# DeltaNet attention and a multiplicative FFN on one core: the 1382 hand-listed steps put in a new order

## The chip, the cores and the metric

The kernel runs on one core of one Trainium2 chip. The metric is the device time of one execution in microseconds (us), lower is better. It is given as the median of several runs; the profile is one further execution. PE stands for TensorE's products, PEld for its weight loads, DVE for VectorE, ACT for ScalarE, POOL for GpSimd and SP for SyncE, which issues nearly all DMAs here.

## The reference

```python
def _attn_ref(q, k, v, beta):            # (4, 8, 768, 48) each, beta (4, 8, 768)
    k_n = k / (np.linalg.norm(k, axis=-1, keepdims=True) + 1e-06)
    state = np.zeros((B, H, D, D))
    for t in range(S):
        kt, vt, bt = k_n[:, :, t], v[:, :, t], beta[:, :, t, None]
        y[:, :, t] = np.einsum('bhd,bhde->bhe', q[:, :, t], state)
        v_old = np.einsum('bhde,bhd->bhe', state, kt)
        state = state + bt[:, :, :, None] * np.einsum('bhd,bhe->bhde', kt, vt - v_old)

x = y.transpose(0, 2, 1, 3).reshape(3072, 384)
a, b = x @ w1, x @ w2                    # (384, 1024) each
out = ((a * b) @ w3) @ w_out             # (1024, 1024), (1024, 384)
```

All values are fp32; w1, w2, w3 and w_out arrive as float64.

## The kernel before

**Stages.** The 768 tokens are cut into 12 chunks m of 64, handled in pairs j (or units u) of two. All 4 batches and 8 heads of a chunk are worked on together, so its products are many small ones, with at most 64 rows and 64 columns of weights, side by side in the 128x128 array. The FFN's products are large ones with 128x128 weights. Since (h @ w3) @ w_out = h @ (w3 @ w_out), `fold` multiplies the two weights once. Each part of the program is a Python generator; one call of it up to its next `yield` is a **step**. `ORDER` is a text that names the part of each step from first to last, so "the third c5" in it is the third step of `chain(5)`. Every engine runs its instructions in the order in which the steps issue them (`in_text_order`): nothing is moved at run time, and an instruction that waits holds up all behind it on its engine.

**The names in `ORDER`:**

- k, q, v (L1223 and after): load a chunk of keys, queries or values by SP. K, Q (`by_tensor`, L369): transpose them by TensorE, then two steps that copy the results out of PSUM by DVE or ACT. From chunk 4 on p (`load_perm`, L261) issues 16 DMAs in two steps and d (`by_vector`, L355) transposes in four steps on DVE.
- g (`squares`): four times a square on POOL and a sum on DVE, then a small product that adds across halves; N (`norms`): some fifteen short DVE instructions and another such product. beta: its load and transposition.
- s (`scores`, for chunks 0 and 1 `first_scores`): products of keys with keys and queries in two halves, each read by DVE into U (L463 or L420) and PT (L474); h (`first_queries`) is the second half's work for chunks 0 and 1. u (`to_blocks`) stores U to DRAM in four DMAs.
- V (`inverse`): fetches U of a pair as 32x32 blocks (for the first pair a DVE transposition, L505, in its place) and inverts them on DVE in 31 steps of two instructions (L524, L529); the result goes out by DMA (L549), for the first pair by four DVE transpositions (L533).
- e (`corner`): fetches the inverses (eight DMAs; for the first pair a product and two ACT copies), a DVE transposition (L602), a product (the third step; L619), two ACT copies, a second product (the fifth step), two ACT copies.
- c (`chain`): the recurrence. Step 1: product with the state; 2: R on DVE (L706); 3: product with the inverse; 4: X on DVE (L717); 5: product with the keys; 6: the new state on DVE (L738). For chunk 0 steps 1 and 2 fall away.
- y (`outputs`): products for the chunk's result (L777), four ACT copies (L795), and DMAs that fill xT.
- P (`piece`): one piece of a weight: DMA (L838), two ACT instructions (L846, L849), one on DVE (L851), one on POOL (L853), which join the float64 halves into fp32. P0-7 are w_out, P8-23 w3, P24-35 w1 and w2. t (`transpose_w3`): four TensorE transpositions and an ACT copy. f (`fold`): 8 large products in two halves and a copy; f0 needs t0 and t1, f1 t2 and t3, and so on.
- a, b (`ab`, L934; a23 is unit 2, columns 3): product with w1, ACT copy, product with w2, multiplication on DVE. For the last unit a5 is `features` (L1074), a Strassen form on the sums of X and W.
- S (`slab_sums`, POOL; DVE for the last unit), o (L1166; seven products of a Strassen form with the folded weight), x (`result`: ACT and DVE read the banks of o, SP stores). T: sums of the folded weight on POOL.

A token whose generator is already at its end does nothing.

**PSUM.** Two double banks (tag "w") serve the attention's products in turn, four banks (tag "f") the large ones and the transpositions. A step that takes a bank waits until its last content has been read.

**The order before** starts with keys and scores, then mixes weight pieces, V0 and `fold`; from about 100 us on it alternates between runs of `ab` or single products of `o` and small products of e, c, s and y.

Of the kernel before, what the change touches and what calls it, by code (L numbers as in the profile page):

```python
# [1358 lines left out]
```

## Time and profile before

| | before |
|---|---|
| time, median of 3 runs | 556.68 us (556.57 to 558.01) |
| span of the profiled execution | 556.1 us |
| `ab`, L934: busy, two groups of 288 records | 106.9 and 106.7 us |
| `o`, L1166: the two largest groups, 320 and 240 records | 57.3 and 42.8 us |
| `fold`, L913 | 43.5 us |
| V on DVE, L524 and L529 with Vb | 43.0 and 43.0 us |
| DMA queue q1 (SP's and ACT's) | 52.56 MB, 46.3% of 16 engines |

A group's line has the source line, engine, operation, tiles and shapes, then busy time and mean length, then the idle time of the engine before these instructions and what ended it. A large matrix product stands as two records. In the chain of waits each piece is a stretch of work that had to end before the next could start.

### The profile page before, as it was taken

To read this page: it belongs to the slowest core of one execution; us is meant where nothing else is said; L and a number is where in the kernel's file an instruction comes from. 1 tells how busy PE (TensorE), PEld (TensorE's weight loads), DVE (VectorE), ACT (ScalarE), POOL (GpSimd) and SP (SyncE) were. 2 spreads that over 40 slices of the span, in tenths; PEclk is the share of its full clock that TensorE was granted. 3 is DMA by queue.
4 is the path that set the end of the run, shared out by engine and by line. 5 is a ranking of instruction groups with operands and counts; after the bars stand their busy time and mean duration, and the time that the engine had idled before them with its cause. 6 is when DMAs were issued, how large, how long until landed. Compare 5 with 4: busy or idle time off the path is not lost.

```text
span 556.1 us, 19932 instructions
## 1 busy us (share of the span) xinstructions
PE 533.6 (96%) x8732; PEld 390.8 (70%) x8732; DVE 343.7 (62%) x800; ACT 145.7 (26%) x291; POOL 169.7 (31%) x213
## 2 busy tenths in 40 slices
PE   6699999999999999999999999999999999989997
...
PEclk9999999999999999999999999999999999999999
...
GB/s 189 339 307 230 158 140 150 128 160 55 96 48 55 119 147 72 67 88 89 122 74 100 70 91 80 126 38 83 51 15 154 26 60 38 18 58 1 0 2 57
DMA packets 191527, 54.22 MB, mean 98 GB/s; under 512 B 178928, under 2 KB 185072, under 8 KB 191440
## 3 DMA queue, kind: packets, MB, share of 16 engines
q1 hardware_dynamic: 189328, 52.56, 46.3%
...
q10 hardware_dynamic: 2112, 0.39, 0.5%
q14 instruction: 19, 0.16, 0.1%
...
## 4 chain that ended last, share of the span: by engine, by line
PE 93%; DVE 3%; issue 2%; DMA 2%; ACT 0%; SPq 0%; DVEq 0%
PE ps_f L934 38%; PE ps_f L1166 20%; PE ps_f L913 7%; PE ps_w L672 6%; PE ps_w L777 4%; PE ps_f L1074 4%; PE ps_w L619 3%; PE ps_w L1074 2%; PE ps_w L451 2%; PE ps_f L369 1%; PE ps_w L457 1%; PE ps_f L904 1%; DMA beta_fm<-in_beta_dram 1%; PE ps_w L409 1%; PE ps_w L1166 1%
## 5 line engine op out<-in xcount | busy, mean ns | idle before, releaser
L934 PE MATMUL ps_f<-xT,w2s 128*128 128x512 f32 (+1 forms) x288 | 106.9, 524 | 0.0
L934 PE MATMUL ps_f<-xT,w1s 128*128 128x512 f32 (+1 forms) x288 | 106.7, 524 | 0.0
L934 PEld LDWEIGHTS ps_f<-xT,w2s 128*128 128x128 f32 x288 | 54.1, 190 | 46.5 <-issue 41.6
L934 PEld LDWEIGHTS ps_f<-xT,w1s 128*128 128x128 f32 x288 | 54.0, 190 | 45.3 <-issue 41.6
L1007 POOL TENSOR_TENSOR ab<-ab 128x256 f32<-128x256 f32 x80 | 56.4, 731 | 78.7 <-DVE ab L950 73.8
L946 ACT COPY ab<-ps_f 128x512 f32<-128x512 f32 (+1 forms) x48 | 24.3, 515 | 134.4 <-PE ps_f L934 130.3
L1166 PE MATMUL ps_f<-w,ab 128*128 128x192 f32 x320 | 57.3, 332 | 1.9 <-DVE osb L1197 1.3
L1166 PEld LDWEIGHTS ps_f<-w,ab 128*128 128x128 f32 x320 | 51.6, 190 | 3.3 <-issue 2.4
L524 DVE TENSOR_TENSOR tb<-Vb,Ub 128x31 f32<-128x31 f32 (+15 forms) x124 | 43.0, 347 | 15.4 <-DMA Ub<-Ud 11.5
L529 DVE TENSOR_TENSOR Vb<-Vb,tb 128x31 f32<-128x31 f32 (+15 forms) x124 | 43.0, 346 | 4.3
L913 PE MATMUL ps_f<-wo,w3T 128*128 128x384 f32 x128 | 43.5, 491 | 0.4 <-ACT w3T L907 0.4
L1166 PE MATMUL ps_f<-room,ab 128*128 128x192 f32 x240 | 42.8, 332 | 0.0
L950 DVE TENSOR_TENSOR ab<-ab,ps_f 128x512 f32<-128x512 f32 (+1 forms) x48 | 27.4, 589 | 24.0 <-PE ps_f L934 24.0
L1166 PEld LDWEIGHTS ps_f<-room,ab 128*128 128x128 f32 x240 | 38.7, 190 | 0.7
L913 PEld LDWEIGHTS ps_f<-wo,w3T 128*128 128x128 f32 x128 | 23.5, 190 | 15.4 <-ACT w3T L907 0.5
L301 POOL TENSOR_TENSOR sq<-ktok 128x384 f32<-128x384 f32 x24 | 19.7, 835 | 43.5 <-DMA out_dram<-osb 16.9
L658 POOL TENSOR_TENSOR vtok<-vtok,n 128x384 f32<-128x384 f32 x24 | 19.8, 832 | 39.5 <-DMA vtok<-in_v_dram 39.5
L635 ACT COPY T<-ps_w 32x512 f32<-32x512 f32 x24 | 13.8, 577 | 67.2 <-PE ps_w L619 46.2
L795 ACT COPY xT<-ps_w 112x256 f32<-112x256 f32 x48 | 14.3, 384 | 65.0 <-PE ps_w L777 61.7
L451 PE MATMUL ps_w<-KQ 48*64 48x128 f32 x320 | 21.9, 274 | 1.8 <-DVE PT L474 1.5
L717 DVE TENSOR_TENSOR X<-ps_w,wt 128x768 f32<-128x768 f32 x12 | 11.5, 956 | 19.4 <-PE ps_w L672 12.9
L1197 DVE TENSOR_TENSOR room<-room,ps_f 128x384 f32<-128x384 f32 (+1 forms) x13 | 7.0, 537 | 26.4 <-PE ps_f L1166 26.4
...
## 6 DMA issues: line engine op xcount, KB each, us to landing
...
```

The costliest lines, as they stand in the source:

```text
L451: pe.matmul(ps[half(z), 0, n : n + 128], lhsT=x[:, 0, :], rhs=x.rearrange("p j t -> p (j t)"), start=True, stop=True,)
L524: dve.tensor_tensor(out=tv, in0=V[:, 0 : s + 1, s : s + 1].to_broadcast([P, s + 1, n]), in1=U[:, s, s + 1 : BS].unsqueeze(1).to_broadcast( ...
L529: dve.tensor_tensor(out=o, in0=o, in1=tv, op=ALU.subtract)
L672: pe.matmul(out(ps, r, h, z), lhsT=lhs(r, h, z), rhs=rhs(r, h, z), start=True, stop=True,)
L777: i = pe.matmul(region(h, z, r), lhsT=lhs, rhs=rhs, start=part[n] not in part[:n], stop=part[n] not in part[n + 1 :],)
L913: pe.matmul(ps[:, 0:DM], lhsT=w3Ts[jc, kc // 4][:, kc % 4 * P : kc % 4 * P + P], rhs=wo(kc), start=(kc == 0), stop=(kc == KF - 1),)
L934: pe.matmul(ps[:].rearrange("p b c t -> p b (c t)"), lhsT=w[:, m, js], rhs=x[:, m, :, c0:c1].rearrange("p b c t -> p b (c t)"), start=(m = ...
L946: act.copy(out=t, in_=ps)
L950: dve.tensor_tensor(out=t, in0=t, in1=ps, op=ALU.mult)
L1007: (dve if u == last else pool).tensor_tensor(out=o_, in0=x_, in1=y_, op=op)
L1074: pe.matmul(ps[:, j, :], lhsT=w[j], rhs=x, start=first and j == 0, stop=j == 1, skip_group_check=not first,)
L1166: pe.matmul(ps[b][:, b, :], lhsT=ab_of(u, HF * f + i, t0), rhs=ws_[w][:, i], start=first and i == 0 and (b == 0 or n == "F"), stop=i == HF ...
```

## The change

The text of `ORDER` is replaced by another arrangement of the same 1382 tokens. Each part's own steps stay in their order; no part, tile, shape or instruction is added or taken away. What moves with a step is all that it issues, its DMAs too. At the start the two chunks of keys come first, weight pieces follow with their four steps together, and K1's copies stand behind P12, P0, P3 and P9. Later, small steps that stood one or two at a time between large products are more often in one row, and large products likewise. The diff, cut to its core (the lines that hold the steps spoken of below):

```diff
 ORDER = """
-k0 g0 g0 g0 K0 V0 g0 k1 P12 K0 K0 beta K1 P0 g0 g0 K1 K1 g0 q1 P12 g0 P12 P12 beta g0 g0 beta N0
-P8 P9 P8 P8 P8 P3 P0 P3 P3 P9 P0 s1 s1 s1 P9 s0 P3 P0 P13 P13 P13 s0 s0 V0 V0 V0 P1 P1 Q1 P1 P9
-Q1 P10 P13 V0 V0 Q1 P1 P10 P2 P2 t0 t0 P2 P4 P4 V0 t1 P2 t1 V0 P4 P4 h1 t4 t4 N0 P6 f0 P7 P10
-P10 P5 t2 t5 P18 V0 V0 P11 P6 V0 P6 P6 N0 P16 P19 V0 P7 P7 P5 P5 P5 q0 V0 t5 h1 P18 f2 P11 V0
...
-t9 v0 V0 P23 f4 f4 t14 f4 t15 t15 P21 P15 P15 t7 q3 V0 v1 Q2 Q2 V0 e0 h0 h0 e0 Q2 g1 e0 g1 t7 g1
-f3 e0 e0 K2 P27 K2 e1 e0 e0 n0 e1 k3 f7 P27 n0 e1 c0 e1 P21 e1 f7 V1 g1 c0 y0 P28 c0 P20 P25 f7
-P20 P20 P29 f3 P33 y0 n1 n1 P21 g1 c0 c1 y0 g1 g1 K2 f3 P28 P28 P28 P34 c1 t13 t13 t12 t12 P25
...
-n3 V1 V1 b2 a00 a00 a05 a05 g2 g2 g2 g2 a06 n2 b1 b1 b0 e2 b0 a06 g2 b3 b3 b7 b7 o0 g2 c2 n3 x0
-e2 e2 g2 g2 o0 d4 e2 g2 e2 g2 o0 S0 S0 S0 e2 c2 d4 S0 S0 e3 S0 S0 x0 S0 S0 S0 S0 e3 e3 S0 S0 d4
...
-S1 n5 n4 a13 a12 a12 a13 V2 e4 a17 e4 a11 g3 g3 g3 g3 a11 Q3 c4 g3 g3 n4 c4 e4 a16 a16 e5 e4 e4
-e4 o1 x1 S1 a17 S1 S1 S1 e5 e5 S1 e5 d6 n5 g3 c4 c4 g3 o1 S1 c4 V3 c4 g3 e5 e5 o1 p7 g3 N3 c5 p7
-x1 S1 x1 S1 y4 S1 y4 c5 o1 d7 d7 d7 d7 s7 s7 k8 g4 s7 s7 s6 s7 s7 u7 s6 s6 s6 s6 s6 c5 S1 c5 o1
...
-V3 e6 g4 a26 a26 a26 a24 d8 a21 n6 c6 e6 a26 d8 e7 a24 e6 e6 p9 g4 g4 g4 s8 N4 s8 a23 a23 s8 e6
-S2 e7 a21 e6 a23 a23 c6 e7 e7 c6 v7 o2 v9 o2 n7 n7 S2 y6 S2 S2 S2 V4 x2 K2 N4 c6 c6 o2 y6 e7 S2
-S2 S2 d9 d9 p10 S2 e7 c7 S2 x2 o2 d9 d9 c7 S2 s8 c7 x2 s8 o2 s8 c7 S2 y7 S2 v8 n8 x2 K1 o2 x2 x2
-u8 Q2 s9 s9 S2 S2 s9 y7 y7 s9 s9 u9 S2 o2 x2 s9 c7 x2 c7 V4 a32 a32 N4 k10 x2 x2 a36 a36 d10 d10
...
-e10 e11 e11 W x4 e11 c10 o4 S4 N5 e11 c10 c10 e11 c10 S4 S4 o4 x4 y10 S4 c11 n11 o4 S4 y10 n11
-c11 c11 c11 S4 S4 o4 y11 x4 S4 y11 y11 S4 x4 o4 S4 x4 x4 x4 x4 x4 o4 x4 a50 a50 a51 X5 a52 X5
...
+k0 K0 k1 K1 K0 K0 g0 g0 g0 g0 V0 g0 g0 g0 g0 P12 P12 P12 P12 beta P0 P0 P0 P0 P3 P3 P3 K1 beta
+beta P9 P9 P9 P9 P3 K1 K1 K1 g0 g0 N0 s1 t4 P13 P13 P13 P13 P1 P1 P1 P1 s1 s1 t4 s0 s0 s0 P2 P2
+P2 P2 P10 P10 P10 P10 t1 t1 t5 t5 V0 V0 q1 Q1 Q1 Q1 f2 h1 P8 P8 P8 P8 t0 V0 V0 V0 V0 V0 P4 P4
+P4 P4 P6 P6 P6 P6 t2 V0 V0 V0 t0 f0 P5 P5 P5 P5 P7 P7 P7 P7 f2 V0 P18 P18 P18 P18 V0 V0 V0 V0
...
+h0 V0 V0 e0 e0 e0 e0 e0 k2 K2 K2 K2 K2 g1 P28 g1 g1 P23 P21 g1 k3 g1 Q0 P26 P20 g1 n0 K3 K3 K3
+e0 e0 e1 P21 t15 t15 f7 f7 e1 e1 e1 P20 t12 g1 g1 g1 P25 q3 P25 P25 P25 P30 v1 P27 P27 P27 P30
+P30 P30 c0 f7 e1 e1 e1 t12 Q3 g1 c0 c0 y0 y0 c0 c1 t13 t13 f6 P27 P35 n1 n1 c1 N1 P26 c1 s2 P29
+Q3 Q3 P35 P35 c1 P24 P29 P29 P24 P24 s2 f6 f6 s2 P33 P33 P31 N1 N1 s2 s2 s2 y1 P31 y1 s3 P32
+P32 s3 s3 s3 k5 y0 y0 P24 b0 b0 s3 s3 P29 b4 b4 P34 P34 P33 u2 u3 c1 b6 b3 b1 b6 b1 y1 P35 P34
...
+T T v2 n2 n2 b1 p4 p4 d4 k4 g2 a04 d4 g2 g2 g2 T T S0 b1 g2 g2 g2 a05 a05 S0 a06 b7 a07 a06 c1
+b7 a07 g2 V1 V1 o0 V1 v3 e2 e2 e2 d4 e2 d4 g2 g2 N2 c2 c2 e2 e2 o0 x0 o0 p5 e3 e3 e3 S0 S0 S0
...
+o1 x1 e4 a14 S1 S1 S1 a17 S1 S1 S1 n4 S1 g3 g3 d6 d6 c4 c4 e5 e4 e4 e4 e5 o1 e5 c4 N3 e5 e5 e5
+c4 c4 c4 y4 y4 c5 n5 S1 o1 x1 c5 c5 p7 d7 p7 d7 d7 d7 N3 c5 v6 n6 s7 s7 s7 s7 s7 s7 o1 s6 s6 p8
+u7 x1 v7 s6 s6 s6 u6 o1 S1 S1 S1 S1 S1 S1 x1 N3 n7 S1 S1 s6 V3 V3 y5 y5 y5 c5 c5 o1 x1 x1 x1 x1
+V3 V3 p8 k9 V3 V3 V3 V3 c6 d8 d8 x1 o1 x1 x1 V3 V3 V3 V3 V3 V3 V3 V3 V3 V3 V3 V3 d8 V3 V3 a22
...
+g4 g4 N4 a22 a22 e6 s8 s8 s8 e6 e7 e7 a26 a26 S2 S2 a23 a23 S2 o2 S2 x2 S2 S2 S2 c6 c6 N4 s8 s8
+s8 u8 o2 c6 c6 y6 y6 p9 p9 e7 c7 e7 e7 v9 S2 n9 e7 o2 x2 c7 N4 d9 d9 V4 S2 S2 S2 S2 p10 k10 o2
+d9 d9 c7 c7 s9 y7 y7 y7 s9 s9 d10 d10 o2 x2 x2 s9 s9 u9 c7 o2 x2 x2 x2 a30 V4 x2 S2 S2 S2 o2 x2
...
+e8 e8 a37 S3 g5 g5 N5 n8 c8 c8 e8 e8 e8 o3 o3 x3 S3 S3 e9 e9 d10 e9 e9 c8 c8 o3 e9 x3 e9 S3 S3
...
+e11 N5 N5 e10 c10 o4 x4 x4 S4 S4 e11 e11 e11 S4 W S4 W S4 S4 c10 c10 c10 S4 S4 S4 S4 S4 S4 S4
+S4 W S4 S4 o4 c11 n11 c11 e11 o4 e11 c11 c11 y10 y10 y11 y11 y11 x4 o4 x4 x4 o4 x4 x4 x4 x4 x4
...
 """
```

More of the change, by code (lines that the diff above doesn't have):

```diff
@@ L76 @@
-c9 y8 y8 K1 S3 S3 c9 c9 o3 N5 o3 x3 s10 d11 s10 s10 y9 s10 s10 d11 d11 d11 S3 S3 W y9 y9 S3 S3
-o3 x3 W s10 x3 x3 s11 s11 s11 s11 s11 u10 u11 V5 S3 S3 x3 x3 o3 x3 x3 a44 s11 v11 V5 a45 V5 V5
-V5 V5 a45 a42 a42 v10 V5 a44 a46 a46 V5 V5 V5 V5 V5 V5 a41 V5 V5 V5 V5 a43 c9 a43 V5 V5 a41 a47
-a47 V5 V5 a44 a44 V5 V5 V5 V5 W V5 a40 a40 a45 V5 a43 V5 a41 V5 V5 V5 V5 a43 a45 a42 a40 a42 c9
-a46 V5 e10 e11 e10 W a41 W a40 c10 n10 n10 c10 e10 N5 a47 e10 e10 W a46 S4 a47 S4 S4 o4 S4 S4 S4
-e10 e11 e11 W x4 e11 c10 o4 S4 N5 e11 c10 c10 e11 c10 S4 S4 o4 x4 y10 S4 c11 n11 o4 S4 y10 n11
@@ new lines @@
+P34 P33 V1 V1 b3 b6 P32 b6 b5 b5 P31 V1 V1 V1 V1 V1 V1 V1 V1 V1 V1 V1 V1 V1 y1 a06 a06 a05 a05
+a03 a03 b7 b7 a00 a00 a07 a07 V1 V1 V1 P31 P32 b0 b0 b4 b4 b3 b3 a01 a01 a01 a02 V1 V1 V1 V1 V1
+a01 V1 a03 a03 V1 V1 V1 a00 a00 b2 a02 b2 a02 a02 V1 V1 V1 V1 V1 V1 V1 b2 b2 b5 b5 a04 a04 a04
+T T v2 n2 n2 b1 p4 p4 d4 k4 g2 a04 d4 g2 g2 g2 T T S0 b1 g2 g2 g2 a05 a05 S0 a06 b7 a07 a06 c1
+b7 a07 g2 V1 V1 o0 V1 v3 e2 e2 e2 d4 e2 d4 g2 g2 N2 c2 c2 e2 e2 o0 x0 o0 p5 e3 e3 e3 S0 S0 S0
+S0 c2 c2 o0 x0 e3 e3 e3 c2 c2 S0 S0 S0 S0 S0 S0 S0 S0 S0 S0 o0 x0 x0 n3 n3 c3 c3 y2 y2 p5 d5 c3
@@ new lines @@
+p11 d11 d11 y9 y9 y9 s10 s10 u10 s10 o3 x3 x3 x3 s11 s11 x3 s11 s11 S3 s11 u11 V5 o3 x3 x3 V5
+V5 V5 V5 V5 V5 V5 V5 V5 a46 a46 a47 a47 v10 a43 a43 V5 s11 V5 V5 V5 V5 V5 V5 V5 V5 V5 V5 V5 V5
+V5 V5 V5 a45 a45 a41 a41 a40 a44 a44 a40 a42 a40 a42 a42 a42 a40 V5 V5 V5 V5 a41 a44 a44 V5 V5
+V5 x3 e10 a41 a45 a46 a46 a43 a43 o4 a45 x4 c9 e10 e10 e10 a47 c9 e10 c10 a47 o4 n10 n10 c10
+e11 N5 N5 e10 c10 o4 x4 x4 S4 S4 e11 e11 e11 S4 W S4 W S4 S4 c10 c10 c10 S4 S4 S4 S4 S4 S4 S4
+S4 W S4 S4 o4 c11 n11 c11 e11 o4 e11 c11 c11 y10 y10 y11 y11 y11 x4 o4 x4 x4 o4 x4 x4 x4 x4 x4
```

44 lines of the change are left out of this document (19 added, 25 removed).

## The prediction, made before the result was known

> **What bounds the kernel now.** I read the page first: engines, slices, chain.
>
> ```profile
> PE 533.6 (96%) x8732; PEld 390.8 (70%) x8732; DVE 343.7 (62%) x800; ACT 145.7 (26%) x291; POOL 169.7 (31%) x213
> PE   6699999999999999999999999999999999989997
> PE 93%; DVE 3%; issue 2%; DMA 2%; ACT 0%; SPq 0%; DVEq 0%
> ```
>
> TensorE (PE) is the bound: it is busy nearly everywhere after the first two slices, and 93% of the chain that ended last is its products. The same products run after the change, so only three things can move: what a change between large and small products costs, what is lost before PE is full, and the stalls behind that. 3% of the chain, some 17 us, is DVE. The span is 556.1; the median of the runs shown is 556.68, so I add 0.6 to a span to get a time.
>
> **Part one: the changes.** I marked every step of both lists that issues products and counted where large (128x128 weights) and small (at most 64x64) ones follow each other: 109 times before, 85 after, so 24 fewer, or 12 round trips. The chain of waits and PE's timeline price a round trip:
>
> ```profile
> 359.31 20.80 PE ps_f L934 x48
> 380.80 2.77 PE ps_f L934 x6
> 435.87 0.87 PE ps_w L672 x64
> ```
>
> ```profile
> 391.57 0.94 PE L672 MATMUL ps_w<-X,ktok 64*48 64x48 f32 x64
> 392.33 0.77 PE L619 MATMUL ps_w<-T,T 33*33 33x32 f32 x64
> ```
>
> Columns of the chain: start, length, what. Eight halves of `ab`, six records each, take 20.80 in one piece; a half alone between small products takes 2.77. With n for a half and d for entering and leaving, 8n+d=20.80 and n+d=2.77, so n=2.576 and **d=0.19**. On the small side a product of `chain` alone takes 0.87, but 392.33-391.57=0.76 when another small one follows: **0.11** more for leaving. Together 0.30 per round trip. Twelve make **-3.6** us. The large side alone would give -2.3; a change that falls where PE waits anyway saves nothing. I take 3.6, since PE waits little.
>
> **Part two: the start.** What PE must issue ahead of the first product of `corner` (e0) I add up from the chain's rows:
>
> ```profile
> 14.90 2.06 PE ps_w L409 x122
> 16.96 4.42 issue
> ...
> 32.45 7.74 PE ps_f L913 x24
> ...
> 40.63 1.04 PE ps_f L369 x64
> ...
> 45.28 0.44 PE ps_f L904 x4
> ...
> 63.09 0.56 PE ps_w L563 x8
> ```
>
> A half of `fold` takes 2.58 (a third of 7.74), four transpositions of w3 0.44, a set of 64 small ones 0.93 (1.04 less the 0.11), a score 2.06. Before: ten halves, fourteen sets of four, seven of 64, two scores and 1.5 for beta and sums, 44.1 us in all. e0 starts at 63.0, so 18.9 us are lost by then. In the new list two more halves and one set less stand ahead of it: 48.8.
>
> ```profile
> 10.13 0.59 ACT L379 COPY KQ<-ps_f 112x512 f32<-112x512 f32 x1 [1.77 <-PE ps_f L369]
> ...
> 16.11 0.68 ACT L846 ACTIVATE w<-raw 128x512 f32<-128x512 f32 x1 [4.27 <-DMA raw<-in_moe_w_dram]
> 16.69 0.66 ACT L849 ACTIVATE raw<-raw 128x512 uint32<-128x512 uint32 x1
> ```
>
> ```profile
> 13.05 0.20 DVE L310 TENSOR_SCALAR seed<-ss 128x32 uint32<-128x32 uint32 x1
> ...
> 16.38 0.19 DVE L334 TENSOR_TENSOR wt<-wt,beta_tok 128x32 f32<-128x32 f32 x1
> ...
> 19.50 1.28 DVE L420 TENSOR_TENSOR U<-ps_w,wt 128x512 f32<-128x512 f32 x2
> ...
> 23.80 2.04 DVE L505 STREAM_TRANSPOSE Ub<-U 128x1024 f32<-128x1024 f32 x1
> ...
> 58.65 4.04 DVE L533 STREAM_TRANSPOSE TT<-ps_w 32x1024 f32<-32x1024 f32 x2
> ```
>
> Before, the inverse V0 starts behind the transposition that ends at 25.84, and DVE works without a gap until 62.69, when e0 is free to go: 36.85 us for 37.6 us of listed instructions (they overlap a little). In the new list 38.7 us of DVE work lie on that stretch, so 38.0.
>
> When does it begin? In the new list K1's copies out of PSUM stand on ACT and DVE behind the weight pieces P12, P0, P3 and P9, so these engines wait there for DMA. The bytes ahead of P9's end are 2.7 MB (k0, k1 0.79, P12 0.52, beta 0.1, P0 and P3 0.39 each, P9 0.52); the page's first slice of 13.9 us moved 189 GB/s:
>
> ```profile
> GB/s 189 339 307 230 158 140 150 128 160 55 96 48 55 119 147 72 67 88 89 122 74 100 70 91 80 126 38 83 51 15 154 26 60 38 18 58 1 0 2 57
> ```
>
> That is 2.6 MB, so P9 lands at about 14.5 and ACT, at 1.3 us per piece, copies K1 at about 16.3-16.9 (10.1 before). But s1's results were not read until 19.50 before. Now DVE has P9, N0 (13.05 to 16.57 above, 3.5) and two small pieces ahead of them: about 21.3. Four copies, two small pieces and the transposition follow: V0 starts at 26.9, 1.1 us later than before, and ends at 64.9. Walking the fold's steps against POOL's pieces (f2's first half begins at 25.5, its second at 34.4), I find PE at e0 at 67.0.
>
> ```profile
> L853 POOL TENSOR_TENSOR w<-w,raw 128x512 uint32<-128x512 uint32 x7 | 9.0, 1292 | 13.6 <-ACT raw L849 5.8 <-DVE w L851 3.6 <-ACT w L846 3.1
> L853 POOL TENSOR_TENSOR wo<-wo,raw 128x384 uint32<-128x384 uint32 x7 | 7.1, 1032 | 3.8 <-DVE tb L524 1.7 <-ACT raw L849 1.4 <-ACT w3T L907 0.6
> ```
>
> These are POOL's pieces ahead of 63 us: count, busy time, mean ns. By DVE alone e0 starts at 65.1 and the loss is 16.3, by the walk 18.2, against 18.9: -0.7 to -2.6. I take **-1.7**. Each us by which P9 lands later than 15 comes back one for one.
>
> **Part three: the stalls behind the start.** Before, the chain leaves PE for pieces of DVE over half a us behind 63 us, with PE waiting:
>
> ```profile
> 95.61 0.69 DVE U L463
> ...
> 246.47 0.69 DVE U L463
> 247.16 0.61 DVE PT L474
> ...
> 249.03 0.69 DVE U L463
> 249.72 0.61 DVE PT L474
> ...
> 492.75 0.56 DVE osb L1197
> ```
>
> They are thirteen, of 0.56 to 0.97 each, and sum to 8.5 us; first, last and the closest four are shown. All these places are arranged anew except the last, where o4's seventh product still follows its sixth directly. What comes instead I worked out from the new list: for each small product that needs a reading by another engine, the lengths of the products in between (those above; a step of `ab` 2.58, in the first unit 1.29, of `o` 2.6) against what the reading needs by these rows:
>
> ```profile
> 67.16 1.18 ACT L635 COPY T<-ps_w 32x512 f32<-32x512 f32 x2 [1.12 <-PE ps_w L619]
> ```
>
> ```profile
> 230.15 5.35 SPq L261 DMA_DIRECT2D kperm<-in_k_dram  x8
> 235.60 5.02 SPq L261 DMA_DIRECT2D qperm<-in_q_dram  x8
> ```
>
> ```profile
> 108.50 0.45 SPq L510 DMA_DIRECT2D Ub<-Ud  x1
> ```
>
> ```profile
> 113.21 0.19 DVE L524 TENSOR_TENSOR tb<-ps_w,Ub 128x31 f32<-128x31 f32 x1 [1.61 <-DMA Ub<-Ud]
> ...
> 137.48 0.20 DVE L529 TENSOR_TENSOR ps_w<-ps_w,tb 128x31 f32<-128x31 f32 x1
> ...
> 147.55 0.71 DVE L602 STREAM_TRANSPOSE T<-TT 128x512 f32<-128x512 f32 x1
> ```
>
> - Corners: two copies (1.2, 1.4 with the handing over) lie between a corner's two products; e2, e4 and e8 now have only 0.9 to 1.1 us of other products there, e5 and e7 0.9, e0 and e1 about 1.1: **2.3** in all.
> - `chain`: c0's and c4's third and fifth steps stand 0.6 to 1.5 us apart around DVE's X of 0.96: **1.0**. s3's second half waits for ACT's reading of y1: **0.7**.
> - V1: between u3 and e2 lie 42.2 us of products. Needed are 8.8 (from u3's first store, 4.1 ahead of the load at 108.50, to 113.21), 25 for the 23.9 us that DVE has on V1's stretch, and up to 10.6 (137.68 to 148.26): 43 to 44.4: **0.7** too little.
> - SP: sixteen issues of a permuted load take 10 us from first to last, landing and two transpositions 3.9 more. p9 now stands behind u8 (2.0), which waits for DVE's reading of s8 (0.7); from there to s9 PE has 14.6 us where 16.6 are needed. p7 before s7 is 1.0 short: **3.0**.
> - The seventh product of `o` needs two readings by DVE (0.56 each) behind the sixth. o1 has c6's 0.9 us between the two: 0.3; o4 has nothing, as before: 1.4. **1.7**.
>
> Together 9.4, so **+0.9** against 8.5; taken as nothing, or all as long as the longest, they are the ends that the rivals below use. DMA issues and queues that I don't name have more cover than before: from u5, u9 and u11 to their corners the products grow from 39.5, 40.3 and 42.9 to 44.6, 47.2 and 44.6 us. Only V3 loses some (49.4 to 45.9, of 44 needed). The steps behind the last product are the same in the same order.
>
> Sum: -3.6 -1.7 +0.9 = **-4.4**; the profiled execution's 556.1 becomes 551.7, with 0.6: **552.3 us**.
>
> **The rivals.**
>
> *Cold products* (554.9). The granted clock of the page is full in every slice, but the first four transpositions of w3 take more than twice the 0.44 of later ones:
>
> ```profile
> PEclk9999999999999999999999999999999999999999
> ```
>
> ```profile
> 24.25 1.03 PE L904 MATMUL ps_f<-ident,w 128*128 128x128 f32 x4
> ```
>
> So until about 25 us products go at half rate. The new list has its first fold, f2, at 25.5 behind a gap of 2 us; if it is still slow it takes 5.2 instead of 2.6: +2.6. Against it: PE has then worked almost without a gap since 17, where before it stood still for 4.4 us until 21.4. The Trainium skill ("TensorE: Matmul & The Clock Gate", Part 1: The HAM clock gate) says that the array runs at half clock until a window of about 3.4 us has been busy, and falls back after an idle one; by that rule f2 would be at full rate. These rows agree with a half rate, the clock row of the page doesn't show it.
>
> *The handoffs are covered* (547.6). If DVE and ACT stand ready at corners, chain, s3 and V1, 4.7 of the 9.4 go. For it: DVE is 62% busy, ACT 26%.
>
> *Chained groups* (560.8, slower). The new list has nine groups of four or more small steps that hang on each other (e0 to e1, c0 to c1, s2 to s3, e2, e4, e5 to c5, c5 to s7, c6 to e7, e8), where before five such stood. I gave them 7.7 us (all but `o`), 0.9 each. The group at 246 to 250 us before lost 2.6 us in four DVE pieces. If each of the nine loses 1.8, because DVE and ACT have other work queued ahead of the reading that PE needs, that is 16.2, or +8.5. From 1.35 us per group on the gain is gone, from 1.55 the kernel is slower by more than a measurement's doubt.
>
> *The changes cost nothing* (555.9): if PE's pauses at them only stand in for waits that come anyway, part one is lost.
>
> **Chances.** 0.3% (1.7 us), about what a measurement of this kernel tells from no change, puts the bounds at 555.0 and 558.4. Forecast 0.40 (550.3 to 554.3, 0.37 faster, 0.03 same where it ends above that); covered 0.23, all faster; chained groups 0.20 (0.17 slower, 0.03 same); cold 0.10 (half faster, half same); nothing 0.07 (0.01 faster, 0.05 same, 0.01 slower). So faster 0.66, same 0.16, slower 0.18. The range takes in the covered case and the chained one up to 1.7 us per group: 547.0 to 560.0.
>
> **What would show it.** Part one: PE's rows of `ab` and `o` beside small ones, with the same 0.19, at 85 places. Part two: first row of V0 at 27, e0's first product at 65 to 67; a first fold that takes over 4 us speaks for cold products. Part three: DVE pieces in the chain at e2, s7, s9 and o1; if the chain has over 15 us of ACT, DVE and DMA behind e0, the groups decide, and with under 5 the handoffs are covered. The prediction is wrong altogether if SP's queue or a late weight piece leaves PE idle for several us at one place.

## The result, and the profile after

The new order takes **595.61 us** (median of four runs, 593.88 to 598.12); the order before took 556.88 in the same session (556.57 to 558.01). The ratio is **1.0687 [1.0647, 1.0727]**: 38.7 us slower, where 4.4 us faster was forecast. The profiled execution took 593.88 us, its span is 592.1 (556.1 before), so the traces have 36.0 us to explain. Of the experiments' runs one of e15 (591.88 us) was in a slower state of the chip and is left out of its median.

The page of the changed kernel: engines, slices of the granted clock, the queue that carries instructions, and the chain's shares.

```profile
PE 547.8 (93%) x8732; PEld 403.3 (68%) x8732; DVE 356.0 (60%) x800; ACT 146.1 (25%) x291; POOL 171.3 (29%) x213
...
PEclk9999978999999999979999979999999999999999
...
q8 instruction: 68, 1.11, 0.8%
...
PE 65%; DVE 8%; DMA 5%; issue 4%; SPq 4%; ACT 2%; DVEq 0%; ACTq 0%
```

The same 8732 records now keep PE busy for 14.2 us more (547.8 against 533.6), and PE stands idle for 21.8 us more (592.1 less 547.8, against 556.1 less 533.6). The granted clock, full in every slice before, dips in four slices. PE's share of the chain fell from 93% to 65%; the rest is spread over many short pieces, and "issue", time in which PE waited for nothing that the profile shows, has twice its former share.

PE's own waits (line that waited, what for: us in total, times, longest), after:

```profile
PE ps_w L777 <- issue: 6.7, 5, 2.4
PE ps_w L672 <- issue: 6.5, 5, 1.9
PE ps_f L369 <- DMA ktok<-in_k_dram: 5.2, 4, 4.0
PE ps_w L409 <- issue: 3.5, 1, 3.5
PE ps_w L619 <- issue: 2.5, 2, 1.3
...
PE ps_f L934 <- DVE ab L950: 2.0, 3, 0.8
PE ps_f L1166 <- DVE osb L1197: 1.6, 2, 1.3
PE ps_f L369 <- DMA raw<-in_moe_w_dram: 1.5, 1, 1.5
...
PE ps_w L563 <- DVE TT L533: 1.1, 1, 1.1
PE ps_w L619 <- DVE T L602: 1.1, 1, 1.1
PE ps_w L457 <- issue: 0.9, 2, 0.5
```

and before, the rows with "issue" (a fourth has 0.3):

```profile
PE ps_w L409 <- issue: 5.4, 2, 4.4
...
PE ps_w L672 <- issue: 0.8, 2, 0.5
PE ps_w L777 <- issue: 0.5, 1, 0.5
```

With the last row of 0.2, "issue" sums to 20.3 us after and 7.0 before. All of L777, L672, L619 and L457 are small products whose data lay ready.

Stretches of the changed kernel in which the granted clock was one half; each row has from:to, us, busy time and count of PE, PEld, DVE, ACT and POOL, clock, DMA share, GB/s:

```profile
73.89:77.30 3.41, 3.41 (x156) 3.41 (x148) 1.68 (x4) 2.09 (x5) 0.46 (x1) 0.50 1.07 187
80.71:84.12 3.41, 3.41 (x7) 1.90 (x6) 0.98 (x3) 2.77 (x5) 2.03 (x3) 0.50 0.93 202
97.78:104.61 6.83, 5.53 (x69) 3.90 (x62) 3.31 (x14) 3.57 (x10) 0.00 (x0) 0.50 0.36 65
258.20:268.44 10.24, 9.76 (x210) 9.24 (x200) 4.31 (x6) 1.19 (x4) 0.00 (x0) 0.50 0.19 34
346.95:357.19 10.24, 8.53 (x191) 8.17 (x180) 3.63 (x7) 3.32 (x8) 0.00 (x0) 0.50 0.72 105
```

PE is busy for 30.6 of these 34.1 us; at full rate the same work would have taken half, so at most 15.3 us are lost here. All lengths are multiples of 3.41. The clock's record in the trace begins only at 29.5 us (25.1 before), and the page of the profile counts the time ahead of it as full. The rows say otherwise: a set of 64 transpositions takes 2.06 us at 27.62 and 1.11 at 43.22. So the half rate of the start lasted 4.4 us longer in the new order, with PE busy: up to 2.2 us more.

**The account.** "Issue" 14.8 us more (20.3, and 1.5 of Q3 that the view gives to a weight piece but that belongs here, as shown below, less 7.0); other waits, all rows of the view together, 17.8 after against 10.0 before, 7.8 more; half rate up to 15.3. Together 37.9, and up to 40.1 with the longer half rate of the start, for 36.0: some 2 to 4 us are left on the other side, and in them lies what fewer changes between large and small products gain.

**What "issue" is.** Queue q8 brought 68 packets of instructions with 1.11 MB, 16.4 KB each, in both kernels. PE has 17,464 instructions, a weight load and a product for each record; 17,464/68 is 257. So a packet is a block of 256 instructions, 128 records. I counted through PE's queue in the trace (loads, products, semaphores and drains): s0's, e0's, Q3's, y0's, c1's and nine later waits of some half a us and more all stand at place 193 or 194 of a block of 256, inside steps whose first products had already run. The chain shows two in a row (start, length, what), and some rows needed later:

```profile
80.76 5.56 DMA raw<-in_moe_w_dram
86.34 4.75 DMA raw<-in_moe_w_dram
...
290.22 33.47 PE ps_f L934 x78
...
324.49 2.77 PE ps_f L934 x6
...
342.73 1.33 PE ps_w L777 x91
344.06 1.68 issue
...
348.12 1.08 PE ps_w L672 x26
349.21 1.19 issue
350.40 1.16 PE ps_w L672 x31
```

y6 had issued 91 of its 96 records and c7 26 of 64 when nothing more came. The theory, called the supply theory below: **PE's instructions come in blocks of 128 records, and a block needs 3 to 5 us to arrive.** A small product takes 13.6 ns in a full set (0.87 us for 64), so a block of nothing else is used up in 1.75 us; with six records of `ab` in it, 2.6 us, it lasts over 4. An order that gathers small products uses up its blocks faster than they come.

The trace also holds the time of each of q8's packets, and it confirms this. In all fourteen waits PE runs on 1.3 to 1.6 us after a packet has landed (from the packets' records; us):

| wait | packet begins | packet landed | PE runs on | later by |
|---|---|---|---|---|
| Q3 | 88.93 | 90.23 | 91.87 | 1.64 |
| y0 | 93.49 | 94.84 | 96.24 | 1.40 |
| c1 | 97.92 | 99.20 | 100.56 | 1.36 |
| y6 | 342.75 | 344.17 | 345.74 | 1.57 |
| c7 | 348.09 | 349.02 | 350.40 | 1.38 |
| c9 | 437.81 | 438.94 | 440.35 | 1.42 |

Where two waits follow each other the next packet begins only after PE has run on: 1.6 us after in Q3, 1.7 in y0, 2.3 in y6.

The Trainium skill ("Runtime: NRT & Kernel Launch", section "Instruction fetch mechanics") has the same blocks of 256 instructions and says that crossing into the next is "mostly hidden". The size agrees; for rows of small products the waits above contradict the second half, and the measurement decides.

### The profile page after: what moved, and what is told of

Same layout as the page of the kernel before. It is cut to its first block, busy times and chain, and to the rows that moved or that the text cites. A ratio compares the mean times of both kernels' runs of the same rounds, so it can differ in the third digit from the quotient of the medians.

```text
span 592.1 us, 19925 instructions
## 1 busy us (share of the span) xinstructions
PE 547.8 (93%) x8732; PEld 403.3 (68%) x8732; DVE 356.0 (60%) x800; ACT 146.1 (25%) x291; POOL 171.3 (29%) x213
## 3 DMA queue, kind: packets, MB, share of 16 engines
q8 instruction: 68, 1.11, 0.8%
## 4 chain that ended last, share of the span: by engine, by line
PE 65%; DVE 8%; DMA 5%; issue 4%; SPq 4%; ACT 2%; DVEq 0%; ACTq 0%
PE ps_f L934 26%; PE ps_f L1166 16%; PE ps_w L672 5%; PE ps_w L777 4%; PE ps_f L1074 4%; DVE tb L524 3%; PE ps_w L1074 2%; PE ps_w L619 2%; DVE ps_w L529 2%; DMA raw<-in_moe_w_dram 2%; SPq L806 1%; PE ps_w L451 1%; PE ps_f L913 1%; PE ps_w L457 1%; DVE Vb L529 1%
## 5 line engine op out<-in xcount | busy, mean ns | idle before, releaser
L1166 PE MATMUL ps_f<-w,ab 128*128 128x192 f32 x320 | 60.8, 347 | 1.6 <-DVE osb L1197 1.6
L1166 PEld LDWEIGHTS ps_f<-w,ab 128*128 128x128 f32 x320 | 56.2, 202 | 4.8 <-issue 3.9
L524 DVE TENSOR_TENSOR tb<-Vb,Ub 128x31 f32<-128x31 f32 (+15 forms) x124 | 44.5, 359 | 17.7 <-DMA Ub<-Ud 14.1
L529 DVE TENSOR_TENSOR Vb<-Vb,tb 128x31 f32<-128x31 f32 (+15 forms) x124 | 46.2, 373 | 4.3
L913 PE MATMUL ps_f<-wo,w3T 128*128 128x384 f32 x128 | 46.7, 517 | 0.4 <-ACT w3T L907 0.2
L658 POOL TENSOR_TENSOR vtok<-vtok,n 128x384 f32<-128x384 f32 x24 | 20.3, 855 | 70.2 <-DMA vtok<-in_v_dram 62.6
L1166 PEld LDWEIGHTS ps_f<-room,ab 128*128 128x128 f32 x240 | 38.7, 190 | 1.1 <-issue 0.3
L913 PEld LDWEIGHTS ps_f<-wo,w3T 128*128 128x128 f32 x128 | 25.1, 203 | 17.3 <-issue 3.2
L706 DVE TENSOR_TENSOR R<-vtok,ps_w 128x768 f32<-128x768 f32 x11 | 10.5, 951 | 26.6 <-PE ps_w L672 23.0
L457 PE MATMUL ps_w<-KQ 48*64 48x64 f32 x640 | 23.0, 220 | 0.9 <-issue 0.9
L524 DVE TENSOR_TENSOR tb<-ps_w,Ub 128x31 f32<-128x31 f32 (+15 forms) x62 | 21.0, 339 | 3.5 <-ACT ps_w L518 2.0
```

The costliest lines, as they stand in the source:

```text
L457: pe.matmul(ps[half(z ^ j), 1, n + C * j : n + C * j + C], lhsT=x[:, 0, :], rhs=x[:, j, :], start=True, stop=True,)
L524: dve.tensor_tensor(out=tv, in0=V[:, 0 : s + 1, s : s + 1].to_broadcast([P, s + 1, n]), in1=U[:, s, s + 1 : BS].unsqueeze(1).to_broadcast( ...
L529: dve.tensor_tensor(out=o, in0=o, in1=tv, op=ALU.subtract)
L913: pe.matmul(ps[:, 0:DM], lhsT=w3Ts[jc, kc // 4][:, kc % 4 * P : kc % 4 * P + P], rhs=wo(kc), start=(kc == 0), stop=(kc == KF - 1),)
L1166: pe.matmul(ps[b][:, b, :], lhsT=ab_of(u, HF * f + i, t0), rhs=ws_[w][:, i], start=first and i == 0 and (b == 0 or n == "F"), stop=i == HF ...
```

## The experiments

Unless said otherwise, a figure like +13.5 us is the difference of medians against the kernel before in the same session. "Handover theory" is the name for the forecast's view that only changes between large and small products, or other engines, make PE wait. In the kernels with extra products, these write to the banks next in turn; in e1, e2, e6 and e7 that overwrites the first product of `chain(6)`, whose values are then not the reference's.

### Small products in a row and spread: e1, e2, e6, e7

In the kernel before, extra small products stand between two products of a24, all eight steps in one row, or one step between each two of eight large halves. Both have the same number of products, so by the handover theory (changes cost, or other engines do) the row should be the cheaper one; by the supply theory the dearer.

```diff
+    def extra(steps, n):
+        for _ in range(steps):
+            ps = two_banks()
+            for i in range(n):
+                z, h = i % 2, i // 2
+                pe.matmul(
+                    ps[half((z + h) % 2), h % 2, D * (h // 2) : D * (h // 2) + D],
+                    lhsT=ident[half(z), half(1 - z)], rhs=ident[half(z), 0:D],
+                    start=True, stop=True,
+                )
+            yield
-V3 a24 a21
+V3 a24 Z Z Z Z Z Z Z Z a21
```

This is e6, with 32 products (64 records) per step and zero weights. In e1 and e2 a step has 64 products that use two diagonal quarters of the array and weights from the identity.

> The kernel before, with 512 extra small products (64x64 weights, 48 columns, nothing waits for them and they wait for nothing) in one row between two large steps, at a24's first and a21's first product (281 us). Handover theory (rows of small steps lose time because DVE and ACT read late): nothing is read here, so the row costs its work, 512 times 13.6 ns (64 products of chain take 0.87) = 7.0, and one round trip of 0.3: +7.3 us. Supply theory (PE gets its instructions in blocks of 256, 128 products, and after the first two or so a block takes 3.4 to 4.6 us, the times between a block's end and the resumption in the changed kernel at 246, 342, 436 and 521 us): four blocks need 13 to 17 us instead of 7, with 1 to 2 waits of over 1 us inside the row, each at place 193 of 256 of PE's queue, and the large products behind it start at half rate (+2): +11 to +18 us.

> The kernel before, with the same 512 extra small products as eight rows of 64, one between each two of nine large steps (273 to 291 us). Handover theory: 7.0 of work and eight round trips of 0.30: +9.4 us, so 2.1 more than in one row. Supply theory: 128 products now take two rows and two large steps, 7.5 us, longer than a block needs, so no wait and no half rate: +9.4 us as well, but 2 to 9 us less than in one row.

e1 took 589.33 us, 1.0577 [1.0549, 1.0605]; e2 590.87, 1.0595 [1.0578, 1.0613]. **A miss**: in two quarters a record took 30.7 ns (31.4 us for 1024), a block 3.93, and PE waited in neither. It says only that a block every 3.93 us can be had. With four quarters the products are nearly as short as the kernel's own:

> As the earlier row, but with products as fast as those of chain: 256 products, each two records, 512 records in all, alternating over the four quarters of the array, zero weights, in one row at 281 us of the kernel before. Earlier the extra products took 30.7 ns per record, a block of 128 records in 3.93, and neither kernel waited. Now 13.6 ns (64 records of chain take 0.87). Handover theory: work of 7.0 and one round trip of 0.3: +7.3 us. Supply theory: 128 records would take 1.75, and a block takes 3.4 to 4.6: one block goes at full speed, each of the other three waits 1.2 to 2.9: the row takes 12 to 16 us, with two or three waits over 1 us at place 193 or 194 of PE's queue, and large products behind it at half rate (+2): +11 to +18 us.

> The same 512 records as eight rows of 64, one between each two of nine large steps of the kernel before (273 to 291 us). Handover theory: work of 7.0 and eight round trips of 0.30: +9.4 us, 2.1 more than in one row. Supply theory: 128 records come once in two rows and two large steps, 7.5 us, longer than a block takes: no wait over 0.5 and no half rate: +9.4 us too, but 2 to 9 less than in one row.

e6 took 570.98 us, 1.0245 [1.0222, 1.0268], **+13.5**; e7 567.75, 1.0197 [1.0173, 1.0221], **+10.3**. PE's timeline of e6 (start, length, instruction, count, and in brackets the idle time before it):

```profile
280.51 2.54 PE L1273 MATMUL ps_w<-ident 64*64 64x48 f32 x159
284.17 2.08 PE L1273 MATMUL ps_w<-ident 64*64 64x48 f32 x128 [1.12 <-issue]
287.90 2.08 PE L1273 MATMUL ps_w<-ident 64*64 64x48 f32 x128 [1.65 <-issue]
292.45 1.62 PE L1273 MATMUL ps_w<-ident 64*64 64x48 f32 x97 [2.47 <-issue]
294.00 2.84 PE L934 MATMUL ps_f<-xT,w1s 128*128 128x512 f32 x6
```

and of e7:

```profile
272.85 1.15 PE L1273 MATMUL ps_w<-ident 64*64 64x48 f32 x64
273.93 2.84 PE L934 MATMUL ps_f<-xT,w2s 128*128 128x512 f32 x6
```

These products read nothing that another engine writes, and yet PE stops after each 128 records, a block. From start to start the blocks take 3.73 and 4.55 us, for 2.08 us of work. Spread, the same products wait nowhere: one half of `ab` per 64 records is cover enough. The three waits sum to 5.24 us, which with 8.3 us for the 512 records (16.3 ns each) is the +13.5. Each ends 1.5 to 1.6 us after a packet has landed, as above. The row was forecast by the supply theory at 11 to 18, by the other at 7.3. That e6 would add 2 us of half rate didn't come true: the clock stayed full here.

### The same kernel again, and shifted by blocks: e3, e5, e8

e5 is the changed kernel unaltered. e3 puts 2 steps of 32 extra products, e8 2 of 16, into two waits of PE at 10 and 13 us (K1's copies, s1's weights), where PE has time for them.

```diff
-P3 K1 beta beta
+P3 K1 Z beta beta
-N0 s1 t4
+N0 Z s1 t4
```

> The changed kernel with 64 extra small products, 32 of them where PE waits at 10.4 us and 32 where it waits at 12.8 us, so that every later block of 256 instructions ends 64 products earlier in the program. Supply theory: the waits inside steps stay at place 193 of 256 of PE's queue and so move by 64 products; those of over 1 us inside y6 (344.06), c9 (438.47) and y11 (523.06) leave these products and stand half a block ahead or behind; the sum of such waits (24 us) stays within a third, and the time within 8 us of the changed kernel's. Handover theory: the waits stay at the same products, and the time grows by 0 to 2 us.

> The changed kernel unaltered, beside the others of this call on one chip, as their measure: both theories 593 to 600 us (four runs so far: 593.9 to 598.1); the waits inside steps at the same places (e0, c0, c1, e4, c4, y6, c7, c9, y11), if they come from the order of the steps.

> The changed kernel with 32 extra small products, 64 records and 128 instructions of PE with their weight loads, half of them where PE waits at 10.4 us and half where it waits at 12.8 us (the earlier run had twice as many, a whole block, and so moved nothing). Every later block of 256 now ends 64 records earlier in the program. Supply theory: the waits stay at place 193 or 194 of the queue and leave the products where they stood: those of over 1 us inside y6, c9's third step and y11's second half go from there, others appear half a block away. Handover theory: they stay at the same products, at place 65 or 66 of the queue. The time: both within 8 us of the unaltered changed kernel.

e3 took 602.54 us (1.0818 [1.0789, 1.0846]), e5 600.69 (597.08 to 604.3, expected 593 to 600; 1.0777 [1.0714, 1.0839]), e8 602.3 (1.0803 [1.0759, 1.0847]). The changed kernel itself thus moves by some 5 us between sessions, and I don't read smaller differences between these three. e3 is a null test by mistake: its 128 records are just one block, so all places stay, and so did the waits. e8's 64 records shift every place by half a block, and its trace shows which waits hang on the product and which on the place:

```
wait                      new order: step, place  e8: step, place
for a semaphore           f5 to e0, 230           same product, 102
                          a16 to a15, 21          same product, 149
                          o4 sixth/seventh, 68    same product, 196
"issue", or Q3's          e0, Q3, y0, c1, c3,     K3, c0, c1, s3, e2, y2, e5,
                          s4, e4, c4, y6, c7,     y4, c5, e7, y7, o3, y8, y9,
                          c9, y10, y11: 193, 194  y11 elsewhere: 193 to 195
```

y6's and c9's waits are gone, and y2, c5, e7 have new ones of 2.29, 2.77 and 1.61 us. This **settles that the block sets the place of the wait**, not the data, an engine or a transfer of data: behind the two extra steps nothing changed but where the blocks begin. Q3's wait left Q3 too. It had stood behind weight pieces in the chain (the two DMA rows of 80.76 and 86.34 above), and looks there like a late transfer.

### A row in the kernel before, and rows broken up in the new one: e9, e4, e10

e9 moves two products of o2 behind c7's third step in the kernel before. That gathers 436 small records and takes two round trips away.

```diff
-N4 c6 c6 o2 y6 e7
+N4 c6 c6 y6 e7
-c7 S2 x2 o2 d9 d9 c7 S2 s8 c7 x2 s8 o2
+c7 S2 d9 d9 c7 S2 s8 c7 o2 x2 o2 x2 s8 o2
```

> The kernel before with one row formed as the change forms them: the third and fourth product of o2 (319.7 and 324.2 us) moved behind c7's third step, so that y6, c6's last, e7's second, c7's first, a half of s8 and c7's third product, 436 records, stand in one row. Two round trips less. Handover theory: -0.6 for the round trips, and c7's first and third product wait about 0.25 each for DVE: -0.1 to +0.3 us. Supply theory: the third and fourth block of that row would come 1.5 to 2 us after the one before instead of 4, so each waits 1 to 2.5 at place 193 or 194 of PE's queue: +2.5 to +5.5 us, with 1 to 2 on top where PE's clock then falls.

It took 562.69 us, 1.0100 [1.0064, 1.0135]: **+5.0**, inside the supply theory's 2.5 to 5.5, where the other gave at most 0.3. The timeline has two new waits:

```profile
326.87 1.03 PE L672 MATMUL ps_w<-S,KQ 48*64 48x48 f32 x56 [1.28 <-issue]
...
330.65 1.40 PE L672 MATMUL ps_w<-R,TT 64*64 64x48 f32 x41 [0.71 <-issue]
```

They sum to 1.99; the clock was then at one half for 6.82 us with PE busy for 6.11 of them, up to 3.1 us more. This trace is of the slowest of the six runs (568.14 us), its span 10.3 us over that of before: 4.3 of these are lost ahead of the moved steps, where the orders are equal (y0's wait is 1.30 there instead of 0.53, with a window at half rate behind it), and 5.9 in the moved stretch. So the harm can be made in the good order with one row.

The reverse was to mend the new order. e4 moves one product of o2 forward, between y6 and e7; e10 moves products of o1, o2 and o3 in three places.

```diff
-y6 y6 p9 p9 e7 c7 e7 e7 v9 S2 n9 e7 o2 x2
+y6 y6 p9 p9 o2 e7 c7 e7 e7 v9 S2 n9 e7 x2
```

> The changed kernel with one step of 1382 moved: the third product of o2, which stood behind e7's second product, stands between y6 and e7, so the row of 384 small products from c6's last to e7's second (342 to 352 us) becomes two of 192 with 2.6 us of large products between. Supply theory: the waits inside y6 and c7 (1.68 and 1.19) go or shrink to under 0.5 each, and o2's third step runs at full rate again (5.1 to 2.9): -4 to -7 us. Handover theory: e7's readings and c7's have the same products to cover them as before but for o2's step, and y6 does not hang on e7: -1 to +1 us.

> The changed kernel with three of its rows broken up by moving single steps: o1's third to seventh product one or two places earlier (e5, c4, y4, c5, s7 at 250 to 290 us), o2's third between y6 and e7 (342 us), o3's fifth to seventh between y8, c9, y9 and s11 (434 to 455 us); the x and S steps that hang on them go along. Supply theory: the waits at place 193 or 194 in these three stretches (10.6 us in the second profile of the changed kernel, 7.6 in the first) fall to less than half, and the half-rate products behind them (some 4 us) mostly go: 6 to 12 us less than the changed kernel (595.6 and 600.7). Handover theory: the readings have other products to cover them, not more: -2 to +1 us.

**Both missed.** e4 took 600.16 us, 1.0768 [1.0706, 1.0829], no better than e5 where the supply theory gave 4 to 7 us; the -1 to +1 of the other theory fits the time. In its place it did something: from the second product of o2 to a30 went 30.1 us instead of 33.4 (33.6 in e5), and c7's wait is gone; y6's stayed (1.40), and y7 got one of 1.67. e10 took 606.86, 1.0876 [1.0843, 1.0909], worse than e5. "Issue" in the three stretches (243 to 470 us) fell from e5's 11.0 to 6.4, but the steps moved forward now wait themselves: 3.2 us for xT's DMA at `ab`, 2.5 for osb and 2.1 for `ab` on POOL at `o`. Breaking a row up needs large products that are ready, and the new order has used them elsewhere: from 243 to 290 us alone some 1150 small records, nine blocks, have seven products of `o` between them.

### A wait alone: e12

In the kernel before PE waits behind a22 for 4, and behind a47 for 12 copies of a tile onto itself by ACT. No block is short here.

```diff
+    def pause(ns_):
+        for n in ns_:
+            for _ in range(n):
+                act.copy(out=ident[:], in_=ident[:])
+            ps = two_banks()
+            for z in range(2):
+                pe.matmul(
+                    ps[half(z), 0, 0:D], lhsT=ident[half(z), half(1 - z)],
+                    rhs=ident[half(z), 0:D], start=True, stop=True,
+                )
+            yield
-a22 a22 V3 a24
+a22 a22 Y V3 a24
-a47 a47 V5 V5 a44
+a47 a47 Y V5 V5 a44
```

> The kernel before with two pauses of PE between large products: behind a22's first product (278.4 us) and behind a47's first (442.1), PE has to wait for four and for twelve extra ACT copies of the identity onto itself, each estimated at 0.3 us (0.37 for 128x256), some 2.1 and 4.3 us of waiting, with two tiny products after each. No row of small products is near. If waits lower PE's clock: the large products behind the long pause, perhaps behind the short one, take twice their 0.43 for 3.4 to 6.8 us: 6.4 for the pauses and 1.7 to 5 more: +8 to +11 us. If it is rows of small products as such: full rate behind both, +6 to +7 us.

e12 took 567.27 us, 1.0188 [1.0152, 1.0224]: **+9.6** (8 to 11 forecast), for 6.42 us of waits. PE's timeline:

```profile
279.19 0.32 PE L1274 MATMUL ps_w<-ident 64*64 64x48 f32 x4 [1.92 <-ACT ident L1271]
...
446.99 0.42 PE L1274 MATMUL ps_w<-ident 64*64 64x48 f32 x4 [4.50 <-ACT ident L1271]
447.34 4.38 PE L934 MATMUL ps_f<-xT,w2s 128*128 128x512 f32 x6
451.56 2.74 PE L934 MATMUL ps_f<-xT,w1s 128*128 128x512 f32 x6
```

and windows behind both waits, in the columns used above:

```profile
279.80:283.20 3.40, 3.40 (x5) 1.35 (x4) 3.26 (x9) 0.00 (x0) 0.00 (x0) 0.50 0.12 20
283.30:286.70 3.40, 3.40 (x9) 1.52 (x8) 3.13 (x10) 0.69 (x2) 0.00 (x0) 1.00 0.71 89
...
447.06:450.48 3.42, 3.42 (x8) 1.70 (x9) 0.43 (x2) 0.00 (x0) 0.00 (x0) 0.50 0.02 5
450.50:453.90 3.40, 3.40 (x9) 1.52 (x8) 1.97 (x5) 0.00 (x0) 0.00 (x0) 1.00 0.00 0
```

Each wait, the short one too, is followed by one window of 3.4 us at half rate: a half of `ab` takes 4.38 and the next 2.74. That is some 1.6 us on top of each wait, and it **shows that waits of PE can bring the half rate**, not the order as such. Not each wait does: behind c9's wait of 1.88 us in the changed kernel the clock stayed full. The Trainium skill ("TensorE: Matmul & The Clock Gate", Part 1: The HAM clock gate) has windows of about 3.4 us and a fall to half the clock after an idle one. The window's length agrees; a wait of 1.92 us, shorter than a window, was enough here.

### Where along the kernel: e11, and e13 to e18

These mixes follow the new order up to a place and then run the remaining steps in the order before.

```diff
-h0 V0 V0 e0 e0 e0 e0 e0 k2
+h0 V0 V0 e0 P28 P27 k2 P23
```

This is e11's seam, behind e0's first product; the others' lie at the times in the labels.

> A mix: the changed order up to and with e0's first product, then all steps that are left in the order of the kernel before. It prices the start alone. By the forecast (part two): -1.7 us. By the traces: e0's first product comes at 72.3 with 55.5 us of products done, against 63.0 with 50.8, so 16.8 lost against 12.2: +4.6 us, of which the rest gets nothing back: 561 to 563.

> A mix: the changed order up to b0 (117 us; one load of keys, k5, left to later), then what is left in the order of the kernel before. By the loss against the same products done in the trace of before (30.8 against 15.0 us): +15 to +18, since the start alone measured +7.1 where the trace gave +4.6. Supply theory: the 8 to 11 beyond the start are the waits at place 193 or 194 in e0, e1, c0 and c1 (78 to 100 us) and the half rate behind them. Theory of late weight pieces and SP's queue (the chain of the changed kernel has 10.3 us of weight pieces at 81 to 91 us): the same time up to here, but PE's waits would stand where a product needs a late weight, not at a place of the queue.

> The same mix with the seam at a17's second product (241 us; the loads k4 and k5 trade places). From 117 to 241 us the changed order has long runs of ab and few rows; the chain of waits has 30 us of DVE, ACT, DMA and SP there (V1, e2, p4, the transfers of y3). Supply theory: one wait of 0.9 inside c3 and small ones: 2 to 4 more than the mix before it, +17 to +22. Theory of SP and DMA: that chain is PE's time, 10 us or more on top: +25 to +30.

> The same mix with the seam at a22 (290 us). The rows of e4, c4, y4 and c5 are in it (1152 small records with seven steps of o between them, 246 to 288 us). Supply theory: the loss goes from 38.0 to 48.3 in the trace, from 19.6 to 23.4 before: 6 to 9 more than the mix before it, +24 to +30.

> The same mix with the seam at a30 (372 us). From 290 to 334 us there are only ab products, from 342 to 362 the rows of y6, e7, c7 and y7. Supply theory: 6 to 9 more than the mix before it, all of it behind 342 us: +31 to +38.

> The mix once more, with the seam at a35 (378 us) in place of a30. In the one at 372 the seam itself made a wait: three sums of S2 came late, o2's last product stood for 6.8 us with 6.8 us of half rate behind it, some 11 us that belong to neither order. Here these sums stand ahead of the seam. Loss at this point in the traces: 57.5 against 24.9. Supply theory: 6 to 9 more than the mix at 290 us (+25.4), all from the rows between 342 and 365 us: +31 to +37.

> The mix with the seam at a46 (455 us). From 378 to 417 us there are only ab products, from 417 to 455 the rows of e8, c8, y8, c9 and y9. Loss in the traces: 61.8 against 26.5. Supply theory: the wait inside c9 (1.9 to 2.7) and one window at half rate, 3 to 5 more than at 378 us: +34 to +41, so that what is left to the end (y10, y11, o4) costs under 5.

| new order up to | us | ratio | us over before |
|---|---|---|---|
| e0 (e11) | 564.78 | 1.0124 [1.0097, 1.0151] | 7.1 |
| 117 us (e13) | 572.60 | 1.0282 [1.0221, 1.0342] | 15.0 |
| 241 us (e14) | 579.39 | 1.0402 [1.0342, 1.0463] | 21.8 |
| 290 us (e15) | 582.21 | 1.0414 [1.0347, 1.0481] | 24.6 |
| 372 us (e16) | 604.87 | 1.0830 [1.0789, 1.0870] | 47.3 |
| 378 us (e17) | 594.09 | 1.0672 [1.0632, 1.0713] | 37.6 |
| 455 us (e18) | 596.77 | 1.0764 [1.0690, 1.0839] | 40.3 |

The loss isn't at one place. The intervals are some 3 us wide to either side, so a step of a few us from one row to the next is not resolved. e11 contradicts part two of the forecast (a gain of 1.7), and lies above the 561 to 563 worked out from the traces. The stretches that the account loads with waits and half rate cost most: 7.9 us from e0 to 117, 13.0 from 290 to 378. The totals of e13, e15 and e18 fell where the supply theory put them; e17 only just missed the 37 at the top. The steps between fit less well: 2.8 from 241 to 290 and 13.0 from 290 to 378, where 6 to 9 were expected of each. e14 was inside its range for the total, but the stretch from 117 to 241 cost 6.8 instead of 2 to 4; its trace shows "issue" of 0.78 and 1.26 and waits for DVE of 0.55, 1.13 and 1.13 there. **e16 missed**, by an artefact of the seam: the last product of o2 stands right behind slab sums that had been spread out before and waited 6.84 us for POOL to make them, a product ahead of it 1.33 us for DVE, and half rate followed. The seam six us later (e17) doesn't have this. No mix beats the order before.

## Why the prediction was wrong, step by step

**The frame failed first.** "The same products run after the change, so only three things can move" left out a fourth: how fast PE's instructions arrive. In the sum it has no term. Its mark was in a row that I quoted and used as a loss without asking what it was, `16.96 4.42 issue`. Behind 22 us the old order has so little of it (1.6 us) because it puts a large product beside nearly every set of small ones. By the account, supply is 14.8 of the 36.0 us, and half rate up to 15.3 more; 27.3 of its 34.1 us come directly behind such waits (the stretches at 97.78, 258.20 and 346.95, behind y0's, c4's and y6's).

**Part one's price held; its gain of 3.6 wasn't measured by itself.** In the new chain thirteen halves of `ab` take 33.47 and one alone 2.77 (rows above): 13n+d=33.47 and n+d=2.77 give n=2.558 and d=0.21, against 0.19. e7 gives the round trip: +10.3 us less 8.3 for its 512 records (16.3 ns each in e6: 2.08 us for 128), 2.0 for eight round trips, 0.25 against 0.30; the interval of e7 allows 0.17 to 0.50. The forecast's 3.6 fits the 2 to 4 us that the account leaves over, which is too coarse to show it. So a change does cost something where PE has nothing to wait for; whether the 24 of this order fell in such places, as the rival "the changes cost nothing" doubts, stays open.

**Part two was right up to K1's copies, then wrong.** DVE's timeline in the new order:

```profile
16.46 1.31 DVE L310 TENSOR_SCALAR seed<-ss 128x32 uint32<-128x32 uint32 x1
...
22.37 1.28 DVE L420 TENSOR_TENSOR U<-ps_w,wt 128x512 f32<-128x512 f32 x2
25.83 1.29 DVE L420 TENSOR_TENSOR U<-ps_w,wt 128x512 f32<-128x512 f32 x2 [2.17 <-PE ps_w L409]
...
27.63 2.04 DVE L505 STREAM_TRANSPOSE Ub<-U 128x1024 f32<-128x1024 f32 x1
31.30 0.43 DVE L851 TENSOR_SCALAR w<-w 128x512 uint32<-128x512 uint32 x1 [1.62 <-ACT w L846]
32.35 0.19 DVE L524 TENSOR_TENSOR tb<-ps_w,Ub 128x31 f32<-128x31 f32 x1 [0.62 <-ACT ps_w L518]
...
60.93 1.75 DVE L851 TENSOR_SCALAR w1s<-w1s 128x512 uint32<-128x512 uint32 x1
...
68.30 3.94 DVE L533 STREAM_TRANSPOSE TT<-ps_w 32x1024 f32<-32x1024 f32 x2
```

K1's copies ran at 16.27 to 16.83 (forecast 16.3 to 16.9), and s1's results were read at 22.37 (21.3). Then s0 waited 3.5 us for instructions on PE (before, 4.4 at 16.96), and DVE 2.17 us for s0's results, so the transposition ahead of V0 ended at 29.67 (26.9). From there to the end of V0's last transposition 42.6 us passed instead of 38.0: DVE waited 1.62 and 0.62 us for ACT, which had weight pieces ahead of V0's copies, so that V0's first row came at 32.35, and weight pieces of its own were stretched to 1.50 and 1.75 us. V0 ended at 72.2 (64.9). On PE, f2's first half began at 29.61 (forecast 25.5) and its second at 37.49 (34.4), and PE itself reached e0 only at 71.2, then waited 1.1 for DVE: e0 began at 72.3 (65 to 67). The step that failed was taking DVE's pieces end to end as long as in the old order, and PE as waiting for data alone; with it went the whole gain of 1.7, and e11 measured a loss of 7.1 in its place.

The cold rival's cost didn't come, its premise did: products ran at half rate until 29.5 us.

```profile
27.62 2.06 PE L369 MATMUL ps_f<-ident,X 64*48 64x64 f32 x64
```

f2's first half took 2.85 us, not 5.2, because it began 4.1 us later than forecast; in e11 it began at 29.42, 0.5 us ahead of the full clock there, and took 3.06. That is luck for the forecast, not a refutation: the half rate fell on the 64 transpositions above (1.11 later) instead. The argument against the rival, that PE has worked almost without a gap since 17, failed too: s0 waited until 24.69.

**Part three was nearly right in its sizes and still not the point.** Forecast were 9.4 us of handovers behind e0; PE's waits for other engines and transfers there sum to 6.7 (`ab` 2.0, osb 1.6, T 1.1, the rest 0.2 to 0.7 each), among them the seventh product of o4 with 1.3 (1.4). Before, the same view has 4.0, so the step costs 2.7 instead of 0.9.

**The rival "chained groups"** had the right sign and the right places (e0 to e1, e4 and e5 to c5, c6 to e7), but its mechanism, DVE and ACT busy ahead of the reading, is not what the rows show: these groups wait at places of a block. It was also too small, 1.8 us per group against waits of up to 2.4 and half rate behind.

**What was to show it wrong altogether**, "a late weight piece leaves PE idle", seems met by the chain's 10.3 us of DMA at 80.76. e8 says no: that wait moved away with the blocks.

**Open:** what decides when a packet begins. e6's blocks took 3.73 and 4.55 us because the next packet began 1.35 and 2.05 us after PE ran on; its transfer (0.88 and 1.01) and the time from landing to the next product (1.50 and 1.49) hardly differ. Open is also which waits bring half rate. Taken by windows of 3.41 us in step with the clock's own, PE was busy for 41 to 64% of the window ahead of each of the five half-rate stretches in the changed kernel, for 44 and 2% in e12, and for 56 and 65% in e9; c9's wait was split between windows of 79 and 64%, and the clock stayed full. But windows of 57 and 56% at 90.95 and 521.03 us in the changed kernel, and of 61, 61 and 50% in e6, left it full as well, so no limit comes out of this. e6 differs by zero weights around its waits; that was not tried by itself.
